# Loads of sixteen rows per partition in three buffers, three chunks held back, tail stores in halves of four rows

## The chip, the cores and the metric

The kernel runs on one core of one Trainium2 chip. The metric is the device time of one execution, in microseconds. The core has TensorE (PE, with its weight loads as PEld), VectorE (DVE), ScalarE (ACT), GpSimd (POOL) and SyncE (SP), and sixteen DMA engines. Two DMA queues matter here: q0, fed by POOL, and q1, fed by SP. Both run on the same sixteen engines.

## What is computed

```python
# _attn_ref, then _moe_ref on its output; B, N, C = 4, 6208, 256; capacity = 128, F = 1024
qn = q / (np.linalg.norm(q, axis=1, keepdims=True) + 1e-06)
kn = k / (np.linalg.norm(k, axis=1, keepdims=True) + 1e-06)
s = kn.transpose(0, 2, 1) @ qn / tau          # 256 x 256 for each batch
a = softmax(s)                                # over the last axis
x = v @ a                                     # 6208 x 256 for each batch
scores = np.einsum('bsd,d->bs', x, w_gate)
for b in range(B):                            # the 128 rows with the largest scores
    top_idx = np.argpartition(-scores[b], capacity)[:capacity]
    xe = x[b, top_idx]
    ye = np.maximum(xe @ w1, 0.0) @ w2
    out[b, top_idx] = xe + sigmoid(scores[b, top_idx])[:, None] * ye   # other rows: out = x
```

## The kernel before, in words

A batch has 6208 rows of 256 floats. They are cut into six chunks of 1024 rows, eight rows (RPP) on each of 128 partitions, and a remainder of 64 rows. POOL's DMAs bring q, k and v in and turn them from f32 into bf16 on the way (`emit_load`); one such load is one chunk of one tensor, 1 MB read and 512 KB written. Output chunks are written by SP's DMAs from f32 stage buffers (`emit_store`), 1 MB each. Batches are numbered 0 to 3; the code calls the last one L and the one before it E.

For each batch TensorE first makes `g_ps` (L390, column norms of q and k, as products of 64 columns with themselves, two side by side) and `s_ps` (L401, k transposed times q). A chain of small steps makes the softmax (`softmax_stages`), which gives `a_sb` and the scoring vector `aw_sb`. TensorE transposes v in groups of four rows (L500), the result is copied to `vt_sb` (13 buffers, `VT_BUFS`), scored (L547) and multiplied with `a_sb` into `o_ps` (L581, two rows at a time, a "pair"), and ACT copies each pair to the stage (L592).

`select_stages` finds the 128 best rows by a seven-step search on DVE and TensorE (L648, L666), gathers their rows of v (`vg`, L734, an indirect DMA on q0), and runs the small network on them: transposes (L758), rows times `a_sb` in two layouts (L768, L771, both in one PSUM tile), h (L795), y (L818) and `upd` (L822). An indirect DMA (L836, the "scatter") then writes the 128 rows over what the plain stores of that batch have written, so it waits for those stores to land.

Batch E is special: two of its chunks (`LATE`) are computed last of all, after batch L, and get the network's result added by TensorE (L588, with one-hot rows `late_oh`), so their stores may follow E's scatter. In the text a "late pair" is four matmuls of L581 and four of L588.

The order of all work is decided by a planner in the kernel's own Python, by costs and due times. It fixes each engine's program; on the chip, semaphores do the rest. What matters here: POOL executes loads, gathers and scatters in the order in which they were emitted, SP likewise its stores. Each DMA of POOL also waits for the landing of the DMA of POOL eight places ahead. `AHEAD` (12 us of load time by the planner's reckoning) limits how many loads are emitted ahead. Output chunks of batches E and L, and of the last two chunks of batch 1 (`BACK`), are held back: their stores start only when the load called `GATE` has landed, the last but one piece of v of batch L. From then on the DMA engines carry stores alone.

## Time and profile before

| | |
|---|---|
| median of 3 runs | 260.41 us (260.26 to 263.3) |
| the profiled execution | 261.13 us |
| its span in the trace | 259.1 us |
| PE, DVE, ACT, POOL busy | 81%, 38%, 37%, 22% of the span |
| q0 (loads, gathers, scatters) | 38.93 MB, 75.4% of sixteen engines' time |
| q1 (weights, stores) | 27.53 MB, 26.3% of sixteen engines' time |

The share of a queue is the time of its packets over the span times sixteen engines. Packets overlap a little on an engine, so shares of a full stretch read 1.0 to 1.07. "GB/s" counts written bytes; the loads read twice what they write.

### The profile page before, as it was taken

Reading aid. Unit: us, or ns where it says so; the run is one execution under the profiler, and the core shown is the slowest. Engines: PE = TensorE matmul, PEld = TensorE weight load, DVE = VectorE, ACT = ScalarE, POOL = GpSimd, SP = SyncE. Lnnn points to the kernel's source line nnn. Section 1 sums busy time; section 2 is a strip of 40 time slices with the busy share of each in tenths; the row PEclk is TensorE's granted clock in tenths of the full one; section 3 lists DMA queues with packets and bytes.
Section 4 is the critical chain, followed back from the end, with each engine's and each line's share of the span. In section 5 each row is a group of like instructions: output and inputs, shape, how many; then the busy total and the mean of one; then the engine's idle time right before and its main releaser. Section 6 shows DMA issues by size and latency. Waiting matters only on the chain.

```text
span 259.1 us, 8212 instructions
## 1 busy us (share of the span) xinstructions
PE 210.8 (81%) x3657; PEld 172.2 (66%) x3657; DVE 97.3 (38%) x414; ACT 96.3 (37%) x176; POOL 56.3 (22%) x105
## 2 busy tenths in 40 slices
PE   0386658778999895998848999898999999999581
PEld 0265546666876674786636788787878888887471
DVE  0200004367450055544463023546555264765021
ACT  3800003900116565466400021811023197798430
POOL 8241213123113110220204322213205200010201
PEclk9999997999999997999995999999999999999979
DMA  7999999999999999999999999999999996999994
GB/s 239 256 218 213 214 214 213 213 212 213 213 217 294 314 361 324 245 282 300 359 240 214 212 215 211 215 210 214 214 213 209 214 211 186 414 419 410 398 409 199
DMA packets 16852, 66.97 MB, mean 259 GB/s; under 512 B 2097, under 2 KB 3634, under 8 KB 13618
## 3 DMA queue, kind: packets, MB, share of 16 engines
q0 software_dynamic: 12528, 38.93, 75.4%
q1 hardware_dynamic: 4290, 27.53, 26.3%
q8 instruction: 28, 0.46, 0.6%
q14 instruction: 6, 0.05, 0.0%
HBM read 78.91 MB, written 25.95 MB: 405 GB/s over the span
## 4 chain that ended last, share of the span: by engine, by line
DMA 43%; PE 37%; DVE 6%; ACT 5%; issue 4%; POOL 1%; SPq 1%; POOLq 1%; DVEq 0%
DMA k_ch<-in_k_dram 18%; DMA q_ch<-in_q_dram 15%; PE s_ps L401 10%; DMA v_ch<-in_v_dram 7%; PE g_ps L390 6%; PE o_ps L581 5%; PE sc_ps L533 4%; ACT stage L592 3%; DMA out_dram<-stage 2%; PE sc_ps L547 2%; PE vt_ps L500 2%; PE m_ps L666 2%; DVE cmp L648 1%; SPq L604 1%; PE g_ps L581 1%
## 5 line engine op out<-in xcount | busy, mean ns | idle before, releaser
L592 ACT COPY stage<-o_ps 128x512 f32<-128x512 f32 x78 | 44.0, 590 | 60.8 <-PE o_ps L581 59.3
L401 PE MATMUL s_ps<-q_ch,k_ch 128*128 128x256 bf16 x384 | 49.9, 283 | 0.0
L581 PE MATMUL o_ps<-a_sb,vt_sb 128*128 128x256 bf16 (+1 forms) x270 | 39.5, 277 | 2.0 <-ACT stage L592 1.9
L401 PEld LDWEIGHTS <-k_ch 128*128 128x128 bf16 x384 | 36.5, 101 | 6.1
L581 PEld LDWEIGHTS <-vt_sb 128*128 128x128 bf16 (+1 forms) x294 | 26.7, 98 | 8.3 <-issue 4.1
L390 PE MATMUL g_ps<-q_ch 128*64 128x64 bf16 x768 | 18.2, 201 | 13.6 <-DMA q_ch<-in_q_dram 13.6
L390 PEld LDWEIGHTS <-q_ch 128*64 128x64 bf16 x768 | 15.0, 116 | 18.8 <-DMA q_ch<-in_q_dram 15.1
L500 PE MATMUL vt_ps<-ident_b,v_ch 128*128 128x128 bf16 x344 | 24.3, 219 | 2.4 <-ACT vt_sb L516 2.3
L390 PE MATMUL g_ps<-k_ch 128*64 128x64 bf16 x768 | 18.3, 202 | 9.2 <-DMA k_ch<-in_k_dram 9.0
L415 DVE SCALAR_TENSOR_TENSOR junk<-g_ps,ident_h 128x64 f32<-128x64 f32 x16 | 3.6, 224 | 58.2 <-PE g_ps L390 57.7
L500 PEld LDWEIGHTS <-v_ch 128*128 128x128 bf16 x384 | 22.7, 97 | 3.7 <-issue 2.5
L390 PEld LDWEIGHTS <-k_ch 128*64 128x64 bf16 x768 | 15.2, 117 | 13.6 <-DMA k_ch<-in_k_dram 10.3
L243 POOL DMA_DIRECT2D q_ch<-in_q_dram x25 | 13.9, 556 | 45.7 <-PE o_ps L581 11.9
L519 DVE COPY vt_sb<-vt_ps 128x1024 bf16<-128x1024 bf16 x24 | 15.8, 688 | 17.4 <-PE vt_ps L500 17.4
L243 POOL DMA_DIRECT2D v_ch<-in_v_dram x25 | 13.6, 545 | 34.6 <-DMA q_ch<-in_q_dram 18.6
L243 POOL DMA_DIRECT2D k_ch<-in_k_dram x25 | 13.7, 546 | 28.3 <-DMA v_ch<-in_v_dram 13.1
L410 ACT COPY s_sb<-s_ps 128x512 f32<-128x512 f32 x4 | 2.3, 585 | 46.8 <-PE s_ps L401 46.8
L533 PE MATMUL sc_ps<-w_sb,ident_b 128*128 128x256 bf16 x123 | 18.5, 277 | 0.4 <-DVE sc L619 0.4
L648 DVE SCALAR_TENSOR_TENSOR cmp<-sc,wl,tab 128x392 bf16<-128x392 f32 x28 | 17.5, 627 | 1.0
L836 POOL DMA_INDIRECT out_dram<-upd,idx x4 | 4.0, 995 | 50.1 <-DMA out_dram<-stage 40.2
L547 PEld LDWEIGHTS <-vt_sb 128*128 128x128 bf16 (+1 forms) x294 | 10.1, 96 | 5.6 <-issue 2.2
L547 PE MATMUL sc_ps<-aw_sb,vt_sb 128*128 128x2 bf16 (+1 forms) x294 | 11.3, 164 | 3.0 <-DVE aw_sb L479 2.5
(176 smaller groups left out, 262.4 us busy)
## 6 DMA issues: line engine op xcount, KB each, us to landing
out_dram<-stage SPq DMA_DIRECT2D x18, 1024.0 KB, 10.3
q_ch<-in_q_dram POOLq DMA_DIRECT2D x23, 512.0 KB, 15.8
k_ch<-in_k_dram POOLq DMA_DIRECT2D x23, 512.0 KB, 17.1
v_ch<-in_v_dram POOLq DMA_DIRECT2D x23, 512.0 KB, 17.5
out_dram<-stage SPq DMA_DIRECT2D x12, 512.0 KB, 8.3
stage<-in_moe_w_dram SPq DMA_DIRECT2D x2, 1024.0 KB, 7.0
q_ch<-in_q_dram POOLq DMA_DIRECT2D x2, 256.0 KB, 16.2
k_ch<-in_k_dram POOLq DMA_DIRECT2D x2, 256.0 KB, 15.9
```

The costliest lines, as they stand in the source:

```text
L243: ins = nc.gpsimd.dma_start(out=t[:, rows, :], in_=lview(src, b, d)[:, rows, :])
L390: nc.tensor.matmul(g_ps[h * H:(h + 1) * H, 2 * which + cc, :], lhsT=x, rhs=x, start=d == FIRST and s == 0 and cc == 0 and which == 0, stop ...
L401: nc.tensor.matmul(s_ps[:, cc, :], lhsT=kt[:parts, s, cc * P:(cc + 1) * P], rhs=qt[:parts, s, :], start=d == FIRST and s == 0 and cc == 0, ...
L500: nc.tensor.transpose(vt_ps[:, cc, j, :parts], in_=vt[:parts, v0 + j, cc * P:(cc + 1) * P], identity=ident_b[:parts, :parts])
L519: nc.vector.tensor_copy(vt_sb[:, :, :n, :parts], vt_ps[:, :, :n, :parts])
L533: nc.tensor.matmul(t[:, 256:512], lhsT=ident_b, rhs=w1_sb[:, 0, 0:256], start=not sc_open[0], stop=not sc_open[0])
L547: nc.tensor.matmul(sc_ps[:parts, col, :], lhsT=vt_sb[:, cc, j, :parts], rhs=aw_sb[:, cc, :], start=cc == 0 and col == 0, stop=cc == 1 and ...
L581: nc.tensor.matmul(o_ps[:parts, pj, :], lhsT=vt_sb[:, cc, j, :parts], rhs=a_sb[:, cc, :], start=pj == 0 and cc == 0, stop=last and cc == 1 ...
L592: nc.scalar.copy(st[:parts, s0 + pair * 2:s0 + pair * 2 + m, :], o_ps[:parts, :m, :])
L648: nc.vector.scalar_tensor_tensor(out=cmp, in0=sc[:, :, None].to_broadcast([P, NCOL, NTHR]), scalar=wl[:, i, NTHR:NTHR + 1], in1=tab[:, Non ...
L666: nc.tensor.matmul(mps[:, 0:7 * NTHR], lhsT=ones_b, rhs=cmp[:, 7 * h:7 * h + 7, :].rearrange("p s j -> p (s j)"), start=h == 0, stop=h == 6)
L836: ins = nc.gpsimd.indirect_dma_start(out=out_flat[0:(b + 1) * N, :], out_offset=bass.IndirectOffsetOnAxis(ap=idx[:, 0:1], axis=0), in_=upd ...
```

## The change

Loads bring sixteen rows per partition (`LR`): three loads in place of six per tensor and batch, each 2 MB read and 1 MB written, with 3 buffers each for q, k and v (5, 5 and 6 of half the size before). The first load of the program and the last ones of batch L stay cut in pieces (8 and 8 rows; 8, 4 and 4 rows). `VT_BUFS` goes from 13 to 9. Three chunks of batch 1 are held back for the time after `GATE`, not two. While E's scoring vector is ready and E's gather not yet emitted, loads are emitted 6 us ahead, not 12. For batches 0 and 1 the norms are products of 128 columns (one matmul for two). Stores of batch L and of the two late chunks go out in halves of four rows on all 128 partitions, each as soon as its two pairs are staged; before, L's halves were 64 partitions of eight rows, after the whole chunk. Late pairs no longer wait for E's scatter to be emitted, only their stores do. The network's second product (`x_ps`) gets a PSUM tile of its own. For batch L the copy `excl_b` goes to DVE. `calm` lets E's network start at a shorter queue.

```diff
-LR = 8
+LR = 16
@@
-    VT_BUFS = 13
+    VT_BUFS = 9
@@
-    BACK = order[-2:]
+    BACK = order[-3:]
@@ pump
-            if not slots[bucket(u)] or sum(length[key] for key in flying) >= AHEAD:
+            ahead = 6.0 if E in aw_ready and E not in gathered else AHEAD
+            if not slots[bucket(u)] or sum(length[key] for key in flying) >= ahead:
@@ p1_norms
+        if b < TILED:
+            for s in range(r0, r1):
+                for cc in range(2):
+                    x = t[:parts, s, cc * P:(cc + 1) * P]
+                    nc.tensor.matmul(g_ps[:, 2 * which + cc, :], lhsT=x, rhs=x,
...
@@
+    def split(b, ci):
+        return ci < NFULL and (b == L or late(b, ci))
...
-            ins = nc.sync.dma_start(out=view(out, b, ci)[h:P:parts], in_=st[h:P:parts])
+            ins = nc.sync.dma_start(out=view(out, b, ci)[:, rows, :], in_=st[:, rows, :])
@@ select_stages
-        by_act = eng.t["act"] < f + 0.5
+        by_act = b < L and eng.t["act"] < f + 0.5
@@
-                                 rhs=vgt[:, cc, :], start=dc == 0 and cc == 0, stop=False)
+                                 rhs=vgt[:, cc, :], start=dc == 0 and cc == 0, stop=dc == 1 and cc == 1)
+        f = eng.pe(4, P, f)
+        which, x_ps = out_psum(None)
         for cc in range(2):
-            nc.tensor.matmul(mps[:, C:2 * C], lhsT=vgt[:, cc, :], rhs=a_sb[:, cc, :], start=False,
+            nc.tensor.matmul(x_ps[:, 0, :], lhsT=vgt[:, cc, :], rhs=a_sb[:, cc, :], start=cc == 0,
                              stop=cc == 1)
@@
-        yield ("t", hfs[0])
+        yield ("calm", hfs[0])
@@ after the scatter
+        if b == E:
+            for x in waiting:
+                out_store(*x)
@@ calm
-            return L in aw_ready or not acc_dead[0] and len(queue["p1"]) > 24
+            return L in aw_ready or not acc_dead[0] and len(queue["p1"]) > 8
@@ out_store
+        if late(b, ci) and E not in scatter_inst:
+            waiting.append((b, ci, s0))
+            return None
...
+        if split(b, ci):
+            rows, size = slice(s0, s0 + 4), STORE / 2 + 0.03
@@ main loop
-                    r = max(r, late_add[2] if E in scatter_inst else FAR)
+                    r = max(r, late_add[2] if late_add else FAR)
@@
-            cost = {1: 0.2, 2: 0.44, 3: 0.44}
+            cost = {1: 0.2, 2: 0.44, 3: 0.88 if out_at < len(outs) and late(outs[out_at][0], outs[out_at][1][0]) else 0.44}
```

The first place is POOL's program from the last pieces of q and k of batch L to the end (`vg` is a gather, `out_dram<-upd` a scatter; "128x2048" is eight rows per partition). Before:

```order
L243 DMA k_ch<-in_k_dram 128x1024
L734 DMA vg<-in_v_dram,idx 128x256
L243 DMA v_ch<-in_v_dram 128x2048
L245 DMA v_rem<-in_v_dram 64x256
L243 DMA v_ch<-in_v_dram 128x2048 x4
L243 DMA v_ch<-in_v_dram 128x1024 x2
L836 DMA out_dram<-upd,idx 12416x256
L734 DMA vg<-in_v_dram,idx 128x256
L836 DMA out_dram<-upd,idx 18624x256
L836 DMA out_dram<-upd,idx 24832x256
```

The same place of the changed kernel:

```order
L246 DMA k_ch<-in_k_dram 128x1024
L246 DMA v_ch<-in_v_dram 128x4096
L754 DMA vg<-in_v_dram,idx 128x256
L248 DMA v_rem<-in_v_dram 64x256
L246 DMA v_ch<-in_v_dram 128x4096
L246 DMA v_ch<-in_v_dram 128x2048
L246 DMA v_ch<-in_v_dram 128x1024 x2
L754 DMA vg<-in_v_dram,idx 128x256
L856 DMA out_dram<-upd,idx 12416x256
L856 DMA out_dram<-upd,idx 18624x256
L856 DMA out_dram<-upd,idx 24832x256
```

E's gather stood ahead of all v loads of L and now stands behind the first of them; L's gather stood behind the scatter of batch 1 and now stands ahead of it.

The second place is SP's program from the remainder of batch E to the end. Before:

```order
L606 DMA out_dram<-stage_rem 64x256
L604 DMA out_dram<-stage 128x2048 x5
L604 DMA out_dram<-stage 64x2048 x2
L606 DMA out_dram<-stage_rem 64x256
L604 DMA out_dram<-stage 64x2048 x10
L604 DMA out_dram<-stage 128x2048 x2
```

And of the changed kernel:

```order
L626 DMA out_dram<-stage_rem 64x256
L624 DMA out_dram<-stage 128x2048 x5
L624 DMA out_dram<-stage 128x1024 x4
L626 DMA out_dram<-stage_rem 64x256
L624 DMA out_dram<-stage 128x1024 x12
```

The twelve halves of batch L and the four of the two late chunks have four rows on 128 partitions now; the late ones still come last.

The third place is the end of TensorE's program: where the second product of L's network (`y`, L818, now L838) stands against the late pairs (`late_oh`). Before, the last rows are:

```order
L588 LDWEIGHTS late_oh
L588 MATMUL g_ps<-d_b,late_oh 128x256
L818 LDWEIGHTS h_sb
L818 MATMUL o_ps<-w_sb,h_sb 128x256
L818 LDWEIGHTS h_sb
L818 MATMUL o_ps<-w_sb,h_sb 128x256
```

Of the changed kernel:

```order
L838 LDWEIGHTS h_sb
L838 MATMUL g_ps<-w_sb,h_sb 128x256
L598 LDWEIGHTS vt_sb
L598 MATMUL o_ps<-a_sb,vt_sb 128x256
L598 LDWEIGHTS vt_sb
L598 MATMUL o_ps<-a_sb,vt_sb 128x256
L605 LDWEIGHTS late_oh
L605 MATMUL o_ps<-d_b,late_oh 128x256
```

Before, all eight late pairs stood ahead of y, five of them ahead of the network and three between its steps. Now three stand ahead of the network, none between its steps, and five behind y.

## Rows read from the trace of the kernel before

**Rows 1.** The page's slices: share of the sixteen DMA engines in tenths.
```profile
DMA  7999999999999999999999999999999996999994
```
**Rows 2.** Stretches: us, busy time of PE, PEld, DVE, ACT, POOL, PEclk, DMA share, GB/s.
```profile
22.00:38.00 16.00, 10.01 (x272) 8.32 (x264) 0.00 (x0) 0.00 (x0) 3.72 (x7) 1.00 1.06 214
201.00:206.00 5.00, 5.00 (x97) 3.97 (x95) 0.82 (x7) 0.00 (x0) 1.58 (x3) 1.00 1.11 214
220.00:229.00 9.00, 8.93 (x132) 7.37 (x130) 6.78 (x25) 7.01 (x14) 0.00 (x0) 1.00 0.99 411
238.00:250.00 12.00, 8.12 (x69) 6.70 (x66) 1.69 (x8) 4.09 (x7) 1.98 (x2) 0.90 1.03 409
```
**Rows 3.** Stretches in which the DMA engines were not full, and the last.
```profile
214.00:219.00 5.00, 4.63 (x76) 3.99 (x73) 1.54 (x7) 3.74 (x9) 0.00 (x0) 1.00 0.55 131
252.00:255.00 3.00, 1.60 (x15) 1.18 (x13) 1.29 (x4) 0.71 (x3) 0.60 (x1) 1.00 0.52 218
257.00:259.10 2.10, 0.00 (x0) 0.00 (x0) 0.00 (x0) 0.00 (x0) 0.00 (x0) 0.69 0.06 21
```
**Rows 4.** Chain that ended last, its end: start us, us, what.
```profile
245.49 6.38 DMA out_dram<-stage
...
252.25 1.92 issue
```
**Rows 5.** Timeline of L's network: start, us, engine, line, output, count, idle before.
```profile
239.05 0.99 POOL L734 DMA_INDIRECT vg<-in_v_dram,idx  x1 [7.07 <-DMA out_dram<-stage_rem]
246.82 0.28 PE L758 MATMUL vt_ps<-ident_b,vg 128*128 128x128 bf16 x2 [3.88 <-DMA vg<-in_v_dram,idx]
249.16 0.42 DVE L776 CAST xet<-m_ps 128x256 bf16<-128x256 f32 x1 [1.72 <-PE m_ps L771]
250.62 0.78 PE L795 MATMUL s_ps<-xet,w_sb 128*128 128x128 bf16 x8
252.56 1.04 PE L818 MATMUL o_ps<-w_sb,h_sb 128*128 128x256 bf16 x8
253.64 0.48 DVE L822 SCALAR_TENSOR_TENSOR upd<-o_ps,gate,xe 128x256 f32<-128x256 f32 x1 [0.80 <-PE o_ps L818]
```
**Rows 6.** DMA issues of the gathers: us from issue to landing last.
```profile
vg<-in_v_dram,idx POOLq DMA_INDIRECT x4, 7.8
```
**Rows 7.** Timeline: the first held store, the scores' end, ACT's copy, the list of rows.
```profile
217.56 0.33 SPq L604 DMA_DIRECT2D out_dram<-stage  x1
222.49 0.15 DVE sc L617
237.02 0.29 DVE L705 TENSOR_SCALAR oh<-iota_row,m_ps 128x128 bf16<-128x128 f32 x1 [0.60 <-ACT excl_b L703]
238.63 0.15 DVE L728 TENSOR_SCALAR idx<-tok 128x1 int32<-128x1 f32 x1
```
**Rows 8.** Timeline of late pairs, at the full and the low clock.
```profile
238.53 0.38 PE L588 MATMUL o_ps<-d_b,late_oh 128*128 128x256 bf16 x2
238.75 0.38 PE L581 MATMUL o_ps<-a_sb,vt_sb 128*128 128x256 bf16 x2
249.34 0.63 PE L588 MATMUL o_ps<-d_b,late_oh 128*128 128x256 bf16 x2
249.77 0.63 PE L581 MATMUL o_ps<-a_sb,vt_sb 128*128 128x256 bf16 x2
248.00:250.00 2.00, 2.00 (x14) 1.50 (x13) 0.76 (x3) 0.58 (x1) 0.00 (x0) 0.50 1.02 430
```
**Rows 9.** Norms of eight rows, and sixteen products of 128 columns, in the chain.
```profile
169.90 0.92 PE vt_ps L500 x16
195.14 0.62 PE g_ps L390 x32
```
**Rows 10.** POOL around E's gather, and TensorE's last product of q and k.
```profile
195.05 1.00 POOL L734 DMA_INDIRECT vg<-in_v_dram,idx  x1 [6.68 <-DVE tokl L741]
204.96 1.05 PE L401 MATMUL s_ps<-q_ch,k_ch 128*128 128x256 bf16 x8
```

More of the change, by code (lines that the diff above doesn't have):

```diff
@@ L183 @@
     FIRST, LAST = lorder[0], lorder[-1]
+    TILED = 2
     L = B - 1
@@ L209 @@
     units = []
+    aw_ready = {}
+    gathered = set()
     for b in range(B):
@@ L352 @@
     scatter_inst = {}
-    gathered = set()
+    split_inst = []
+    waiting = []
+    THROTTLE = 99
     softmaxes = [0]
@@ L385, in p1_norms @@
         parts = P if d < NL else REM
+        if b < TILED:
[3 more added lines that the diff above has]
+                    nc.tensor.matmul(g_ps[:, 2 * which + cc, :], lhsT=x, rhs=x,
+                                     start=d == FIRST and s == 0 and cc == 0 and which == 0,
+                                     stop=d == LAST and s == LR - 1 and cc == 1 and which == 1)
+            return eng.pe(2 * (r1 - r0), P)
         for s in range(r0, r1):
@@ L411, in softmax_stages @@
         sf = eng.act(2 * C, dep)
[L412 removed]
+        junk = smx.tile([P, P], F32, name="junk")
         nsq = smx.tile([P, 4], F32, name="nsq")
         for i in range(4):
[L415 removed]
+            nc.vector.scalar_tensor_tensor(out=junk[:, 0:width(b)], in0=g_ps[:, i, :], scalar=1.0,
+                                           in1=ident_f if b < TILED else ident_h,
                                            op0=ALU.mult, op1=ALU.mult, accum_out=nsq[:, i:i + 1])
[L417 removed]
+            f = eng.dve(width(b), dep, extra=0.08)
         acc_free[0] = max(sf, f)
@@ L801, in select_stages @@
                 nc.scalar.activation(hv, h_ps, AF.Relu)
-                f = eng.act(4 * P, f)
+                hfs.append(eng.act(4 * P, f))
             else:
                 nc.vector.tensor_scalar_max(hv, h_ps, 0.0)
-                f = eng.dve(4 * P, f)
-            bank_give(which, f)
-            hfs.append(f)
+                hfs.append(eng.dve(4 * P, f))
+            bank_give(which, hfs[-1])
         gate = moe.tile([P, 1], F32, name="gate")
@@ L914, in stage_ready, with after, out_store @@
         return rings.landing(("st",) + key)
-    def out_store(b, ci):
+    def after(later, earlier, reason):
+        tc.add_manual_dep(
+            later.ins, earlier.ins.name,
+            mybir.DependencyInfo(mybir.DependencyClass.Sync, mybir.DependencyReason.DATA), reason=reason)
+    def out_store(b, ci, s0):
+        if late(b, ci) and E not in scatter_inst:
+            waiting.append((b, ci, s0))
+            return None
         dep = stage_done[(b, ci)]
@@ L921, in out_store @@
             dep = max(dep, rings.landing(("scatter", E)))
-        parts = (2 if b == L else 1) if ci < NFULL else 1
-        for h in range(parts):
-            key = ("st", b, ci) if h == parts - 1 else ("st", b, ci, h)
-            issued = eng.issue("sp", 0.42, dep)
-            rings.add(1, issued + 0.65, STORE / parts + 0.009 if ci < NFULL else 0.2, key, 0.45)
-            ins = emit_store(b, ci, h, parts)
-        stored[b].append(key)
-        if not late(b, ci):
-            held[b] -= 1
+        if split(b, ci):
+            rows, size = slice(s0, s0 + 4), STORE / 2 + 0.03
+        else:
+            rows, size = slice(0, RPP), STORE + 0.009 if ci < NFULL else 0.2
+        key = ("st", b, ci) if s0 or not split(b, ci) else ("st", b, ci, 0)
+        if split(b, ci) and len(split_inst) >= THROTTLE:
+            dep = max(dep, rings.landing(split_inst[-THROTTLE][1]))
+        issued = eng.issue("sp", 0.42, dep)
+        rings.add(1, issued + 0.65, size, key, 0.45)
+        ins = emit_store(b, ci, rows)
+        if split(b, ci):
+            if len(split_inst) >= THROTTLE:
+                after(ins, split_inst[-THROTTLE][0], "few stores at a time ahead of the last gather")
+            split_inst.append((ins, key))
+        if s0 or not split(b, ci):
+            stored[b].append(key)
+            if not late(b, ci):
+                held[b] -= 1
         return ins
@@ L951 @@
         if deferred and GATE in load_inst:
-            for b, ci in sorted(deferred, key=lambda d: -d[0]):
-                st = out_store(b, ci)
+            for b, ci, s0 in sorted(deferred, key=lambda d: -d[0]):
+                st = out_store(b, ci, s0)
                 if not gate_done:
                     gate_done.append(1)
-                    tc.add_manual_dep(
-                        st.ins, load_inst[GATE].ins.name,
-                        mybir.DependencyInfo(mybir.DependencyClass.Sync, mybir.DependencyReason.DATA),
-                        reason="stores behind the last loads")
+                    after(st, load_inst[GATE], "stores behind the last loads")
             deferred = []
@@ L1063 @@
                     vt_slots.append(f)
-            if out_at == len(outs) or outs[out_at][1][0] != g[0]:
-                if back(b, g[0]) and not gate_done:
-                    deferred.append((b, g[0]))
-                else:
-                    out_store(b, g[0])
+                if split(b, g[0]) or out_at == len(outs) or outs[out_at][1][0] != g[0]:
+                    s0 = g[1] if split(b, g[0]) else 0
+                    if back(b, g[0]) and not gate_done:
+                        deferred.append((b, g[0], s0))
+                    else:
+                        out_store(b, g[0], s0)
 _INS = ['q', 'k', 'v', 'tau', 'moe_w_gate', 'moe_w1', 'moe_w2', 'moe_capacity']
```

29 lines of the change are left out of this document (14 added, 15 removed).

## Prediction

> **What bounds the kernel now.** I read the page's slices first: the sixteen DMA engines show 9 tenths or more in all slices but the first, one at about 217 us and the last [rows 1]. So the program is DMA-bound nearly throughout, and the next thing to know is the rate and the holes. The table of stretches gives the rate: while loads run alone, 214 GB/s written, which is 428 GB/s read; while stores run alone, 409 to 411 GB/s [rows 2]. A load of eight rows (512 KB written) thus takes 0.524 / 214 = 2.45 us, a chunk's store (1.049 MB) 2.55 us. The holes are two. Between 214 and 219 us the share is 0.55, so 2.25 us are lost: the loads run out, and the held stores start only when `GATE` has landed, the first of them at 217.56 [rows 3, 7]. Between 252 and 255 us the share is 0.52, so 1.44 us are lost [rows 3].
>
> The end of the chain says why the second hole is there: the last store of batch L lands at 251.87, the scatter's waits are over at 252.25, and 1.92 us follow in which nothing in the trace holds POOL [rows 4]. The timeline shows that L's `upd` ends only at 253.64 + 0.48 = 254.12, which is what the scatter was short of [rows 5]. So at the very end two things run side by side: the held stores on the DMA engines, and a chain of latencies from the last load over the scores (222.49), the list of rows (238.78), the gather (239.05, landed 246.82) and the network (254.12) [rows 5, 7]. The chain is about 2 us the longer one. What shortens it beyond 2 us gives nothing, since the stores then end last.
>
> The profiled execution took 261.13 us for a span of 259.1, so 2.0 lie outside the span; it stands 0.7 above the median of 260.41. I work in the span and carry the difference to the median.
>
> **The third chunk held back.** One store of 2.55 us moves behind `GATE`. The bytes before it are fewer by 2.55 us, so `GATE` lands at about 215.0, and everything that hangs on it comes 2.55 us earlier. The stores behind it are longer by the same 2.55 us. L's stores therefore still land at about 251.9, but L's network now ends by 251.6, ahead of them. The scatter can start at 252.3 and the 1.44 us hole closes. This is the term that carries the forecast: **-1.4**. The hole at 214 to 219 stays: the stores still wait for the last but one piece of v, four rows as before.
>
> **The network's chain.** L's list of rows also loses ACT's turn, for which DVE stood idle 0.60 us [rows 7]; a DVE copy takes its place, so I take 0.4. Between xet's end (249.16 + 0.42) and h's start (250.62) 1.04 us pass with a late pair on TensorE, and L771 is waited for too [rows 5]; with both out of the way I take 1.5, between 1.0 and 2.1 (the same again for the pair ahead of L768). E's network lies between the gate and L's scores; its gather now lands behind the first third of v. Before, the scores ended 222.49 - 217.56 = 4.9 us behind the gate; I take 0.5 off, with bounds 0 and 2. L's gather took 7.8 us [rows 6] among stores of 8 KB packets; with packets of half the size its eight rows per engine could wait 8 x 0.16 = 1.3 us less (0.16 is half of 2.55 us over eight packets per engine). Nothing of before shows it, so I take none, with the bound 1.3. L's y then ends at 253.60 - 2.55 - 0.4 - 1.5 - 0.5 = 248.65.
>
> **The late pairs behind y.** Five of eight now follow y on TensorE. A pair is four steps of 0.22 us, 0.88, at the full clock, and four of 0.43, 1.72, at the granted clock of 0.50 (1.2 GHz) [rows 8]. Five take 4.4, to 253.05; ACT's copy adds 0.6, the store's start about 1.4 (the first held store was issued at 217.56, and the engines are full again only behind the stretch that ends at 219 [rows 2, 3, 7]), its 512 KB 1.28: 256.3. Without any wait the data would end at 257.1 - 1.44 = 255.7 (257.1 is where the last stretch's 0.06 of 2.1 us ends [rows 3]). So the late pairs end 0.6 behind that. The bound above is worked out under the second rival, the bound below is no wait; with the gather's possible 1.3 in mind I take **+0.3**.
>
> **Sixteen rows per load.** The stretch 201 to 206 has half loads among its DMAs (2 KB written per packet), 22 to 38 whole ones (4 KB): both 214 GB/s [rows 2]. Larger packets would follow that line: no gain. The fastest stretch shown is 430 [rows 8], 0.5% above the 428 that loads read, which on 72 loads x 2.45 = 176 us would be 0.9. I take half, **-0.4**.
>
> The Trainium skill ("DMA: Bandwidth & Descriptors", Anatomy of one DMA and Measured) gives each DMA a fixed 2.0 us beside its bytes and asks for 1 MiB and more per DMA; by it 36 fewer loads would save up to 72 us. The trace disagrees where several loads are in flight: whole loads and half loads move the same 214 GB/s, so the fixed part is hidden, and by the rows the sum stays as it is.
>
> **The stores' halves.** 409 against 411 GB/s between stretches with halves and whole chunks [rows 2], though those halves still had 8 KB packets. 0.5% of eight chunks (20.4 us) is **+0.1**; nothing to 0.4.
>
> **Edits at nothing.** The 128-column norms cost 0.92 - 0.62 = 0.30 us per eight rows of q or k [rows 9], 12.1 times per batch, 7.3 us in two batches. TensorE is idle 6 us of the 16 between 22 and 38 [rows 2], waiting for loads; were that cover gone, a batch would pay 3.6. Fewer `vt_sb` buffers make the last transposes of a batch wait for its first output pairs, which fall beside loads. The moves on POOL: before, E's gather was issued at 195.05 and held POOL 6.68 us, while the queue still had loads up to the last q and k at 204.96, some 9 us [rows 10]. The changed order puts a load of 4.9 us more ahead of it, so the search may end later by about 5 us before the engines run dry.
>
> **Sum.** -1.4 + 0.3 - 0.4 + 0.1 = -1.4: span 257.7, this execution 259.7, median **259.0**.
>
> **Rivals.** *The loads get faster than any stretch here.* If packets of 8 KB cut a fixed time per packet that halves and wholes of today hide, the loads could gain as much as 2%, 3.5 us of 176, and `GATE` comes earlier by that: 259.0 - 3.1 = 255.9. For it: nothing in the rows; against it: the equal 214 GB/s. *The late pairs become the end (slower than before).* The point from which they decide is y at 255.7 - 1.4 - 1.28 - 0.6 - 4.4 = 248.0. If no step of the network gets shorter, y ends at 253.60 - 2.55 = 251.05 and the data at 258.7, 1.6 later than before: 262.0. If TensorE is at its low clock besides, as it was at 248 to 250 after it had waited 3.88 us for the gather [rows 5, 8], the five pairs take 8.6 and the data end at 262.9: 266.2. For it: TensorE has less to do during the gather, since only three pairs stand ahead of it. Against it: the clock was back when y ran (1.04 for its eight products [rows 5]). *The loads stall.* If E's search slips by more than the cover, POOL stands at E's gather with four loads of v behind it, and each us of it is a us of the program; a slip of 8 us costs 3: 262. For it: larger loads in three buffers, nine `vt_sb`. Against it: POOL waited 6.68 us before and the engines stayed full [rows 1, 10]. *It changes nothing:* the hole of 1.44 us moves to the late pairs: 260.4.
>
> **Chances.** The forecast (257.5 to 260) 0.5; no change (260 to 261) 0.15; faster loads 0.13, of which 0.05 below 255.2; late pairs 0.13, of which 0.04 above 265.6; a stall 0.09, of which 0.03 above 265.6. The range 255.8 to 262.5 leaves out about 0.07 below and 0.12 above. About 2% (5.2 us) is what a measurement of this kernel can tell from no change: faster 0.05, slower 0.07, the same 0.88. The likeliest case alone: 257.5 to 260.
>
> **What the changed profile would show.** The first held store at 215.0, 2.5 earlier; loads still at 214 GB/s in a stretch of loads alone; no hole between L's last store and its scatter, and the scatter right behind that store's landing; L's gather landing in 6.5 to 7.8 us; y before 249; the late pairs behind it at 0.88. Wrong would be a DMA share below 1 between 20 and 210 us, or ACT's last copy of a late pair later than 254.5 with idle DMA engines ahead of it.

## The result, and the profile after

The changed kernel takes 263.9 us (median; 263.69 to 264.39), against 260.6 for the kernel before in the same series: a ratio of 1.0109, 95% interval 1.0069 to 1.0150. It is slower by 1.1%: less than the 2% that the prediction took as the least difference it could tell from none, but with an interval that lies clear of 1, and outside the predicted range of 255.8 to 262.5. The profiled execution took 263.74 us for a span of 261.7.

The page's slices, to be laid beside [rows 1]:

```profile
DMA  7999999999999999999999999999997799999966
```

The hole at about 217 us is no longer seen. Instead there are two sevens at 196 to 209 us, and the last two slices stand at six. Stretches of the changed kernel (columns as in [rows 2]):

```profile
22.00:38.00 16.00, 10.95 (x126) 10.32 (x127) 0.00 (x0) 0.00 (x0) 1.58 (x3) 0.79 1.04 216
200.00:205.00 5.00, 4.88 (x127) 3.85 (x120) 4.00 (x23) 0.20 (x1) 2.07 (x4) 1.00 0.35 67
214.00:219.00 5.00, 4.91 (x81) 4.21 (x78) 2.31 (x9) 3.47 (x8) 0.00 (x0) 1.00 0.96 263
252.00:255.00 3.00, 3.00 (x28) 2.70 (x29) 0.63 (x2) 1.17 (x2) 0.96 (x1) 1.00 0.36 147
257.00:261.70 4.70, 0.00 (x0) 0.00 (x0) 0.00 (x0) 0.54 (x1) 0.00 (x0) 0.99 0.57 227
```

Loads alone run at 216 GB/s (214 before). The hole at 214 to 219 us shrank from 2.25 us [rows 3] to 0.2. But 200 to 205 us, where [rows 2] show full engines, now loses 3.25 us (0.65 of 5). The hole that was to close, 252 to 255 us, grew from 1.44 us to 1.92. And where before almost nothing moved behind 257 us [rows 3], 2.7 us of transfers are left. (Holes are counted against a share of 1.00. Full stretches of loads read up to 1.11, as [rows 2] show, and not only up to 1.07, so these losses are lower bounds.)

The first hole has its cause on POOL. Timeline of DVE, POOL and SP around E's search and gather, first held store, and the end of L's scores:

```profile
183.17 0.15 DVE L637 TENSOR_REDUCE sc<-sc_ps 64x1 f32<-64x2 f32 x1 [0.44 <-PE sc_ps L564]
202.50 0.15 DVE L748 TENSOR_SCALAR idx<-tok 128x1 int32<-128x1 f32 x1
202.93 1.00 POOL L754 DMA_INDIRECT vg<-in_v_dram,idx  x1 [16.68 <-DVE tokl L761]
204.43 2.32 POOL L246 DMA_DIRECT2D v_ch<-in_v_dram  x4
216.32 2.26 SPq L624 DMA_DIRECT2D out_dram<-stage  x2
223.70 0.15 DVE L637 TENSOR_REDUCE sc<-sc_ps 64x1 f32<-64x2 f32 x1 [0.44 <-PE sc_ps L564]
```

POOL stood 16.68 us at E's gather (6.68 before [rows 10]) with one remainder and four loads of v behind it. The gather went out 7.9 us later than before, and 7.2 of these are the start of the search, at 183.17. In the kernel before, the search began at 176.00, and the last transposes ahead of it stood on TensorE at 173.62:

```profile
173.62 1.05 PE L500 MATMUL vt_ps<-ident_b,v_ch 128*128 128x128 bf16 x16
176.00 0.15 DVE L617 TENSOR_REDUCE sc<-sc_ps 64x1 f32<-64x2 f32 x1 [0.44 <-PE sc_ps L547]
```

TensorE of the changed kernel at that place:

```profile
175.26 0.61 PE L517 MATMUL vt_ps<-ident_b,v_ch 128*128 128x128 bf16 x8
175.70 1.04 PE L598 MATMUL o_ps<-a_sb,vt_sb 128*128 128x256 bf16 x8
176.57 0.61 PE L517 MATMUL vt_ps<-ident_b,v_ch 128*128 128x128 bf16 x8
...
179.18 1.05 PE L598 MATMUL o_ps<-a_sb,vt_sb 128*128 128x256 bf16 x8
180.06 0.61 PE L517 MATMUL vt_ps<-ident_b,v_ch 128*128 128x128 bf16 x8
180.51 1.04 PE L598 MATMUL o_ps<-a_sb,vt_sb 128*128 128x256 bf16 x8
181.39 0.61 PE L517 MATMUL vt_ps<-ident_b,v_ch 128*128 128x128 bf16 x8
```

Here transposes of E's last groups (L517) and output pairs (L598, which free `vt_sb`) take turns, and norms of the next batch come between (177.64 to 179.18, left out). Before, two groups were transposed at one go. With nine buffers the tenth group of a batch has to wait until a pair has used up one of the first nine.

The second hole and the end: timeline of L's network, with the scatters of batch 1 (241.01), E (248.39) and L (253.98), and ACT's last copy of a late pair:

```profile
239.71 0.99 POOL L754 DMA_INDIRECT vg<-in_v_dram,idx  x1 [32.96 <-DVE idx L748]
241.01 1.00 POOL L856 DMA_INDIRECT out_dram<-upd,idx  x1 [0.30 <-issue]
247.34 0.29 PE L778 MATMUL vt_ps<-ident_b,vg 128*128 128x128 bf16 x2 [4.29 <-DMA vg<-in_v_dram,idx]
248.39 0.97 POOL L856 DMA_INDIRECT out_dram<-upd,idx  x1 [6.37 <-DMA out_dram<-upd,idx]
251.16 1.39 PE L838 MATMUL g_ps<-w_sb,h_sb 128*128 128x256 bf16 x8
252.59 0.48 DVE L842 SCALAR_TENSOR_TENSOR upd<-g_ps,gate,xe 128x256 f32<-128x256 f32 x1 [0.44 <-PE g_ps L838]
253.98 0.96 POOL L856 DMA_INDIRECT out_dram<-upd,idx  x1 [4.62 <-DMA out_dram<-upd,idx]
256.96 0.58 ACT L609 COPY stage<-o_ps 128x512 f32<-128x512 f32 x1 [0.29 <-PE o_ps L605]
```

Two scatters waited for the landing of the one before. And SP waited for E's scatter with the late stores behind it (waits of SP, 236 to 260 us: total, times, longest):

```profile
SPq L624 <- DMA out_dram<-upd,idx: 8.0, 1, 8.0
```

Both signs that the prediction had named as wrong stand in these rows: a share below 1 between 20 and 210 us, and a last copy of a late pair later than 254.5 with idle engines ahead of it.

So three suspects stood: **A**, the nine `vt_sb` buffers make E's scores late, hence the hole on POOL and a later network of E; **C**, the late pairs behind y set the end; **D**, the scatter of batch 1 moved behind L's gather, every scatter waits for the one before, and the late stores wait for E's. The rival of A was the load size, the rival of all of them the third chunk itself. Times of different series are compared by their ratio to the kernel before, which took 260.6 to 261.8 in them.

### The profile page after: what moved, and what is told of

It is laid out like the page before. It is cut to its first block, busy times and chain, and to the rows that moved or that the text cites. A ratio compares the mean times of both kernels' runs of the same rounds, so it can differ in the third digit from the quotient of the medians.

```text
span 261.7 us, 7347 instructions
## 1 busy us (share of the span) xinstructions
PE 215.6 (82%) x3235; PEld 183.7 (70%) x3235; DVE 95.4 (36%) x411; ACT 101.3 (39%) x179; POOL 40.0 (15%) x74
## 3 DMA queue, kind: packets, MB, share of 16 engines
q0 software_dynamic: 8064, 38.93, 72.7%
## 4 chain that ended last, share of the span: by engine, by line
DMA 42%; PE 25%; issue 23%; ACT 3%; POOL 2%; DVE 2%; POOLq 0%; ACTq 0%
DMA q_ch<-in_q_dram 31%; DMA v_ch<-in_v_dram 9%; PE o_ps L598 6%; PE s_ps L417 6%; PE g_ps L406 4%; DMA vg<-in_v_dram,idx 3%; ACT vt_sb L533 2%; PE vt_ps L517 1%; ACT stage L609 1%; PE m_ps L686 1%; PE sc_ps L564 1%; PE sc_ps L550 1%; POOL v_ch L246 1%; PE o_ps L816 1%; PE o_ps L605 1%
## 5 line engine op out<-in xcount | busy, mean ns | idle before, releaser
L598 PE MATMUL o_ps<-a_sb,vt_sb 128*128 128x256 bf16 (+1 forms) x278 | 40.0, 277 | 0.9 <-ACT stage L609 0.6
L417 PEld LDWEIGHTS <-k_ch 128*128 128x128 bf16 x384 | 37.2, 100 | 4.8
L598 PEld LDWEIGHTS <-vt_sb 128*128 128x128 bf16 (+1 forms) x294 | 27.4, 99 | 7.3 <-issue 3.0
L517 PE MATMUL vt_ps<-ident_b,v_ch 128*128 128x128 bf16 x336 | 25.7, 223 | 5.6 <-ACT vt_sb L533 3.4
L517 PEld LDWEIGHTS <-v_ch 128*128 128x128 bf16 x384 | 23.8, 99 | 7.9 <-issue 4.8
L398 PE MATMUL g_ps<-q_ch 128*128 128x128 bf16 x192 | 14.0, 234 | 15.8 <-DMA q_ch<-in_q_dram 15.8
L398 PEld LDWEIGHTS <-q_ch 128*128 128x128 bf16 x192 | 12.3, 105 | 17.1 <-DMA q_ch<-in_q_dram 16.3
L398 PE MATMUL g_ps<-k_ch 128*128 128x128 bf16 x192 | 16.2, 258 | 8.4 <-DMA k_ch<-in_k_dram 8.4
L398 PEld LDWEIGHTS <-k_ch 128*128 128x128 bf16 x192 | 14.8, 119 | 9.4 <-DMA k_ch<-in_k_dram 9.4
L536 DVE COPY vt_sb<-vt_ps 128x1024 bf16<-128x1024 bf16 x16 | 11.0, 691 | 25.4 <-PE vt_ps L517 25.4
L533 ACT COPY vt_sb<-vt_ps 128x1024 bf16<-128x1024 bf16 (+1 forms) x23 | 19.7, 925 | 0.8 <-PE vt_ps L517 0.7
L754 POOL DMA_INDIRECT vg<-in_v_dram,idx x4 | 4.0, 1005 | 104.2 <-DVE idx L748 87.5
L690 DVE TENSOR_REDUCE cnt<-m_ps 128x8 f32<-128x56 f32 x28 | 6.1, 217 | 19.7 <-PE m_ps L686 19.7
L246 POOL DMA_DIRECT2D q_ch<-in_q_dram x15 | 8.7, 578 | 26.5 <-DMA v_ch<-in_v_dram 13.1
L246 POOL DMA_DIRECT2D k_ch<-in_k_dram x15 | 8.3, 554 | 26.8 <-DMA v_ch<-in_v_dram 11.7
```

The costliest lines, as they stand in the source:

```text
L246: ins = nc.gpsimd.dma_start(out=t[:, rows, :], in_=lview(src, b, d)[:, rows, :])
L398: nc.tensor.matmul(g_ps[:, 2 * which + cc, :], lhsT=x, rhs=x, start=d == FIRST and s == 0 and cc == 0 and which == 0, stop=d == LAST and s ...
L417: nc.tensor.matmul(s_ps[:, cc, :], lhsT=kt[:parts, s, cc * P:(cc + 1) * P], rhs=qt[:parts, s, :], start=d == FIRST and s == 0 and cc == 0, ...
L517: nc.tensor.transpose(vt_ps[:, cc, j, :parts], in_=vt[:parts, v0 + j, cc * P:(cc + 1) * P], identity=ident_b[:parts, :parts])
L533: nc.scalar.copy(vt_sb[:, :, :n, :parts], vt_ps[:, :, :n, :parts])
L536: nc.vector.tensor_copy(vt_sb[:, :, :n, :parts], vt_ps[:, :, :n, :parts])
```

## Experiments: one suspect at a time

### The order of loads and E's gather on POOL

```diff
-            ahead = 6.0 if E in aw_ready and E not in gathered else AHEAD
+            ahead = AHEAD
```

> One edit against the changed kernel: loads are emitted 12 us ahead at all times, so one more v load of sixteen rows (4.9 us) stands ahead of the gather of batch 2 on POOL. Theory A (POOL standing at that gather until 202.9 us dries the DMA engines, 3.3 us lost between 198 and 208): the hole closes, the first held store is issued at about 213 instead of 216.3, and the time falls by 2 to 3 us to about 261; the late pairs behind y still end last. Theory B (larger loads and fewer buffers hold the loads back of themselves): the hole stays, only later, and the time stays within 0.7 us of 263.9.

Measured: 264.53 (264.29 to 264.88), ratio 1.0109 (1.0061 to 1.0156). E's gather still goes out at 203.00, but fewer loads stand behind it:

```profile
200.00:205.00 5.00, 4.88 (x130) 3.85 (x122) 4.00 (x22) 0.20 (x1) 2.00 (x3) 1.00 1.03 211
250.00:252.00 2.00, 1.93 (x21) 1.54 (x18) 0.61 (x2) 1.06 (x3) 0.00 (x0) 0.77 0.19 66
258.02 0.59 ACT L609 COPY stage<-o_ps 128x512 f32<-128x512 f32 x1 [0.29 <-PE o_ps L605]
```

Theory A gave a gain of 2 to 3 us, and there is none. The hole is shut (1.03), and the first held store starts at 213.30, 3.0 us earlier. Not one of these 3 us reaches the end: L's scores end at 224.35 (223.70 with the hole), and the engines run empty at 250 us instead, while late pairs are computed until 258. The hole was real, but it was not what ended last.

### The late pairs ahead of L's network

```diff
+                if self.b == L and out_at < len(outs):
+                    return FAR
```

(in `Chain.ready`, under the step that waits for the gather)

> One edit against the changed kernel: the network of the last batch is emitted only when all eight late pairs are, so all stand ahead of it on TensorE, in the 7.6 us in which it waits for the gather. Theory C (the five late pairs behind y end the program: last copy at 257.5, data at 260.0): the hole of some 2.5 us at 251 to 254 closes, the data end at about 258 and the time falls by about 2 us to 262. If the end were set by the stores alone, it stays at 263.9. If the pairs make the network late, the scatter is later than 254.0 and the gain is smaller.

Measured: 263.88 (263.01 to 265.95), ratio 1.0102 (1.0034 to 1.0171). The last copy of a late pair starts at 247.25, 9.7 us earlier than in the changed kernel, and still nothing is gained, where theory C gave 2 us. Stretch, POOL and SP's wait:

```profile
252.00:254.00 2.00, 0.54 (x5) 0.23 (x4) 0.61 (x2) 0.00 (x0) 0.00 (x0) 1.00 0.09 37
249.54 0.97 POOL L856 DMA_INDIRECT out_dram<-upd,idx  x1 [7.73 <-DMA out_dram<-upd,idx]
SPq L624 <- DMA out_dram<-upd,idx: 8.5, 1, 8.5
```

The finished late chunks lie in their stages and wait for E's scatter, which waits for that of batch 1. That speaks for D.

### The scatter of batch 1 ahead of L's gather

```diff
-            return max(...) + (0.5 if L in gathered else 3.0)
+            return max(...) + (0.5 if L in gathered else -6.0 if b < E else 3.0)
```

> Of the changed kernel only the order on POOL at the end is changed: the scatter of batch 1 is issued ahead of L's gather, as in the kernel before, instead of behind it. Theory D (each scatter waits for the landing of the scatter before it, E's late stores wait for E's scatter, so a scatter moved behind L's gather makes the hole of 2.5 us between 250 and 254): the scatter of E is issued by 244 instead of 248.4, the DMA share of 250 to 254 is above 0.85 instead of about 0.45, and the stores are through about 2 us earlier as far as the late pairs let them. Theory C (the three late pairs and more behind y set the end by themselves): the hole closes, ACT's last copy stays at 257.0, and the time stays within 0.6 us of the changed kernel's 263.9. D and no C: 261.9. If D is wrong, the scatter of E stays at 248 or the hole stays with the scatter early.

Measured: 264.92 (263.92 to 265.45), ratio 1.0129 (1.0084 to 1.0175). E's scatter is out at 242.70, and the end is now the late pairs':

```profile
242.70 0.99 POOL L856 DMA_INDIRECT out_dram<-upd,idx  x1 [2.22 <-DMA out_dram<-upd,idx]
258.68 0.59 ACT L609 COPY stage<-o_ps 128x512 f32<-128x512 f32 x1 [0.29 <-PE o_ps L605]
```

The hole does not close but moves back: 250 to 252 us stand at 0.94, 252 to 254 at 0.48, 254 to 256 at nothing.

So C and D hide each other: the late stores need both the late pairs and E's scatter, and whichever is left holds them.

### Two suspects, and all three

The first two edits together:

> Both edits. If A and C hold and are separate, the gains add: 263.9 - 3 - 2 = about 259, under the kernel before (260.6), and the engines are full from 20 us to the scatter but for the hand-over from loads to stores. If they share one hole, the time is that of the better one, 261 to 262.

Measured: 261.30 (260.67 to 262.15), ratio 0.9994 (0.9970 to 1.0018): 1.15% below the changed kernel, where each edit alone gave nothing. What is left is D: E's scatter at 248.98, and 250 to 252 us at 0.19.

All three edits:

> All three suspects are taken out of the changed kernel: the output pairs no longer go ahead of the transposes of E (hole at 200 to 205 us), the late pairs stand ahead of L's network, and the scatter of batch 1 ahead of L's gather. The first two together gave 261.3 with a hole left at 250 to 252 us (share 0.19) and E's scatter at 248.98. Theory D: the hole closes, E's scatter is out by 245, and what is left is the last scatter's wait: 259.3 to 260.2, at or below the kernel before (260.6). If the scatter order is worth nothing beside the other two: 261.3 again.

Measured: 259.64 (259.36 to 260.08), ratio 0.9938 (0.9915 to 0.9960), faster than the kernel before. Its stretches:

```profile
250.00:252.00 2.00, 1.65 (x18) 0.95 (x14) 1.03 (x4) 0.76 (x3) 0.00 (x0) 1.00 1.03 422
252.00:255.00 3.00, 0.00 (x0) 0.00 (x0) 0.37 (x1) 0.00 (x0) 0.97 (x1) 1.00 1.00 403
```

The engines are full from 250 to 255 (245 to 250 stand at 0.80), and no late pair is computed behind 250.

## Experiments: the buffers, the loads and the third chunk by themselves

### Thirteen buffers, and the control

```diff
-    ST_BUFS = 9
-    VT_BUFS = 9
+    ST_BUFS = 8
+    VT_BUFS = 13
```

> The changed kernel with 13 buffers for the transposed rows, as before the change, and 8 instead of 9 for the output tiles, which makes room for them. Theory A (nine buffers make the last four transposes of a batch wait for its output pairs, so E's search starts 7 us late and POOL stands at E's gather with loads of v behind it): E's search starts at about 176 instead of 183, its gather is issued near 195.5 instead of 202.9, the DMA share of 200 to 205 is above 0.9 instead of 0.35, the first held store is at 213 to 214 instead of 216.3, and the scatter of batch 1 is ahead of L's gather again. The third chunk's gain then shows: 260 if nothing else ends it, 262 to 262.5 by theory C, since the late pairs still follow y (as in the kernel with loads of eight rows, 263.5). If the output tiles are the scarce thing instead, the time is 264 or more.

Measured: 261.26 (260.00 to 263.44), ratio 0.9991 (0.9951 to 1.0031). E's search starts at 175.44, its gather goes out at 195.93, the first held store at 214.30, and the planner by itself puts the scatter of batch 1 (231.15) ahead of L's gather (236.68). Theory A holds, and the order behind D is gone with it. That order needs the third chunk too: with nine buffers and two chunks (last run of this section) the planner also puts the scatter of batch 1 first (235.29 against 240.90). C remains, as expected: the last late pair's copy starts at 255.79, and 252 to 254 us stand at 0.14.

The control, output tiles alone:

```diff
-    ST_BUFS = 9
+    ST_BUFS = 8
```

> A control: the changed kernel with 8 output tiles instead of 9 and its 9 buffers for the transposed rows. With 13 of these and 8 of those it took 261.3. Theory A (the buffers of the transposed rows): 263.5 to 265, the hole at 200 to 205 us stays. If the gain came with the output tiles and the order that they bring: 261.3.

Measured: 264.15 (263.49 to 265.33), ratio 1.0105 (1.0052 to 1.0157), with 200 to 205 us at 0.43. The output tiles did not bring the gain.

### The nine buffers in the kernel before

```diff
-    VT_BUFS = 13
+    VT_BUFS = 9
```

> The kernel before with 9 buffers for the transposed rows instead of 13, and nothing else. Its planner then puts E's gather behind five loads of v instead of ahead of them. Theory A: E's search starts at 181 to 184 instead of 176.0, its gather is issued after 201 instead of 195.05, E's network and L's list of rows come later, L's gather at 240 or later instead of 239.05, and the time is 261.2 to 262.5. If the buffers cost nothing, as the prediction had it: the search starts at 176 and the time is 260.6.

Measured: 265.41 (263.69 to 266.05), ratio 1.0136 (1.0083 to 1.0189). That is more than either theory gave. Search, E's gather, first held store, end of L's scores, L's gather, last scatter and the stretch ahead of it:

```profile
188.69 0.15 DVE L617 TENSOR_REDUCE sc<-sc_ps 64x1 f32<-64x2 f32 x1 [0.44 <-PE sc_ps L547]
209.94 1.00 POOL L734 DMA_INDIRECT vg<-in_v_dram,idx  x1 [8.26 <-DVE tokl L741]
217.27 0.33 SPq L604 DMA_DIRECT2D out_dram<-stage  x1
225.64 0.15 DVE L617 TENSOR_REDUCE sc<-sc_ps 64x1 f32<-64x2 f32 x1 [0.46 <-PE sc_ps L547]
242.14 1.00 POOL L734 DMA_INDIRECT vg<-in_v_dram,idx  x1 [2.06 <-DVE idx L728]
258.11 0.98 POOL L836 DMA_INDIRECT out_dram<-upd,idx  x1 [14.97 <-DVE upd L822]
252.00:258.00 6.00, 6.00 (x55) 5.03 (x53) 2.16 (x7) 2.72 (x6) 0.00 (x0) 0.79 0.09 36
```

With loads of eight rows the search slips by 12.7 us. The planner had put five loads of v ahead of the gather, so POOL's queue did not run dry; the price is paid at the other end, where the last scatter waits for `upd` and the engines stand still for 5.5 us. The gate is as early as before (first held store at 217.27; 217.56 [rows 7]), yet L's scores end 3.15 us later (225.64; 222.49 [rows 7]), behind E's network, whose y starts at 222.37 instead of 217.41.

### The loads

The kernel before with the large loads and the nine buffers that make room for them:

```diff
-LR = 8
+LR = 16
-    VT_BUFS = 13
+    VT_BUFS = 9
```

> The kernel before with loads of sixteen rows in three buffers, and 9 buffers for the transposed rows, which makes the room; two chunks kept back, no halves, all late pairs as before. Loads at 216 to 217 GB/s instead of 213 to 214 give 1.5 to 2 us over 176 us; theory A takes some back: E's search at 181 or later, a hole at 200 to 205 us where POOL stands at E's gather with loads of v behind it. Theory A: 261.5 to 264. Loads alone, if the buffers cost nothing: 258.6 to 259.2.

Measured: 261.69 (259.69 to 264.77), ratio 1.0014 (0.9985 to 1.0043). That is the lower edge of theory A's range and far from the 258.6 to 259.2 of the loads alone. But the hole that theory A gave is not there (200 to 205 us at 1.05; two loads of v and the remainder stand ahead of E's gather), and the runs spread over 5 us, with the profiled one the fastest of them. E's search starts at 183.34, 5.4 us earlier than with eight rows and nine buffers, so part of the difference to the run above is order, not rate.

The changed kernel with loads of eight rows and 13 buffers:

```diff
-LR = 16
+LR = 8
-    VT_BUFS = 9
+    VT_BUFS = 13
```

> The changed kernel with loads of eight rows and thirteen vt_sb buffers again; all else stays, the third held chunk, the halves of four rows, the 128-column norms, the late rule. Theory A: the search of batch 2 starts at about 176 as before, POOL's wait does not dry the engines, and the hole at 198 to 208 is gone; with six late pairs behind y the end is still later than it need be: 259.5 to 261.5. If the time stays near 264, the loads and buffers are not what cost the time.

Measured: 263.55 (262.16 to 266.58), ratio 1.0073 (1.0039 to 1.0108). No hole at 200 to 205 (E's gather at 195.33), scatter of batch 1 at 228.46; late pairs are copied until 256.0. This is a miss: theory A gave 259.5 to 261.5, and a time near 264 was to clear the loads and buffers. With C still there the run by itself tells neither. Against 0.9991 with large loads and 13 buffers this hints that the large loads are worth something; the cleaner run follows below.

### The third chunk

```diff
-    BACK = order[-3:]
+    BACK = order[-2:]
```

> The changed kernel with two chunks of batch 1 kept back, as before the change; all else of the change stays (loads of sixteen rows, nine buffers, halves, five late pairs ahead of L's network and three behind it). Theory that the third chunk itself costs the time (more late pairs and a scatter behind L's gather): 260.6 or less, as before the change. Theory A (the buffers' hole at 200 to 205, 3.3 us, is there as well): the first held store at 218.5 to 219.5, the time 261.5 to 263, most of the loss stays.

Measured: 264.01 (263.83 to 264.35), ratio 1.0107 (1.0065 to 1.0149), the changed kernel's ratio within 0.0002, and above both forecasts. The first held store is at 218.47, 2.15 us later than with three chunks, and the end does not move. But this pair differs in more than the chunk: the scatter of batch 1 stands ahead of L's gather, three late pairs and not five stand behind y, and E's gather goes out at 204.52 and not at 202.93. The chunk's own price is read from a cleaner pair below.

## Experiments: the same terms in a kernel without the losses

13 buffers and the late pairs ahead of L's network:

```diff
-    ST_BUFS = 9
-    VT_BUFS = 9
+    ST_BUFS = 8
+    VT_BUFS = 13
@@
+                if self.b == L and out_at < len(outs):
+                    return FAR
```

> The changed kernel with 13 buffers for the transposed rows (8 for the output tiles), and with L's network emitted only when all late pairs are. The first edit alone gave 261.3 with a hole of 2.7 us at 250 to 254 (shares 0.49 and 0.14), while ACT's last copy of a late pair ended at 256.4. Theory: those are theories A and C, and D is served by the first edit, since the scatter of batch 1 then stands ahead of L's gather. The hole closes, L's last scatter waits for L's stores only (252), and the time is 258.0 to 259.2, clearly below the kernel before (260.6). Rival, that the late pairs ahead of L's network push y and the last scatter later by as much as they save: 260.5 to 261.5.

Measured: 261.24 (260.26 to 262.38), ratio 0.9994 (0.9968 to 1.0020): a miss. In the profiled execution the end is as it should be (full until 256), but E's gather, which stands ahead of all loads of v there, goes out at 197.77, and 196 to 200 us stand at 0.38: 2.5 us lost on POOL. (With 13 buffers alone it had gone out at 195.93, and the share was 0.85, 0.6 us lost. Both kernels issue the same work in the same order up to there, and E's search began at 175.44 in that execution, at 177.90 in this one, the slowest of its ten: the loss at the gather differs from one execution to the next.) The next run puts the first load of v ahead of that gather, by this edit more:

```diff
-            ahead = 6.0 if E in aw_ready and E not in gathered else AHEAD
+            ahead = AHEAD
```

> As the kernel before in this list, and one load of v more issued ahead of E's gather on POOL. In the kernel with 13 buffers alone POOL still stood at that gather, with the DMA share of 196 to 200 at 0.85, which is 0.6 us. If that hole is on the path: 0.4 to 0.8 less than without this edit, 257.5 to 258.6. If E's network comes later by as much as the loads come earlier (as in the kernel where this edit stood alone): the same or 0.3 more.

Measured: 259.23 (258.92 to 259.29), ratio 0.9914 (0.9875 to 0.9953), faster than the kernel before by 0.9%. I had given the hole 0.4 to 0.8, from an execution that lost little there; it was worth 2.1. From here three terms of the change were undone one at a time.

**Late pairs behind y again** (the two lines of `return FAR` taken out):

```diff
-                if self.b == L and out_at < len(outs):
-                    return FAR
```

> The fastest version so far (259.2) with the late pairs where the change put them, five of them behind y. Theory C by itself: ACT's last copy at 255 to 256 and the DMA engines partly idle at 250 to 254, 260.6 to 261.5. If the late pairs are hidden: 259.2.

Measured: 261.76 (260.89 to 262.56), ratio 1.0014 (0.9986 to 1.0042): 1.0%, 2.6 us slower. 250 to 252 us stand at 0.13, the last copy starts at 256.11.

**Loads of eight rows again:**

```diff
-LR = 16
+LR = 8
```

> The fastest version so far (259.2) with loads of eight rows, as before the change. It measures the larger loads by themselves. By the rates read so far (216 to 217 against 213 to 214 GB/s while loads run alone, 1 per cent of 176 us): 260.5 to 261. If larger packets bring nothing, 259.2; the prediction took 0.4: 259.6.

Measured: 260.76 (260.53 to 261.07), ratio 0.9979 (0.9953 to 1.0005): 0.65%, 1.7 us slower. The edit also brings back the load buffers of before (5, 5 and 6 of half the size) and the cuts of the last loads. Loads alone read 213 GB/s there in the stretch of 22 to 38 us and 215 in the kernel with large ones, but 213 in both from 164 to 190. The first held store is at 214.29 instead of 213.08.

**Two chunks held back again:**

```diff
-    BACK = order[-3:]
+    BACK = order[-2:]
```

> The fastest version so far (13 buffers for the transposed rows, late pairs ahead of L's network, loads ahead of E's gather as before the change; 259.2) with two chunks of batch 1 kept back instead of three. It measures the term that carried the prediction, where nothing hides it. The prediction's theory (the chain behind the gate ends last, so 2.55 us of stores moved behind the gate shorten the end by 1.4): 260.4 to 260.8. Rival (the stores end last there, the third chunk only changes places with them): 259.0 to 259.5. It would be below 258.9 if the third chunk costs something by itself.

Measured: 258.99 (258.66 to 260.48), ratio 0.9921 (0.9893 to 0.9949): the same, by the rival's forecast. First held store, end of L's scores and L's gather, first with three chunks, then with two:

```profile
213.08 1.03 SPq L624 DMA_DIRECT2D out_dram<-stage  x2
221.38 0.15 DVE L637 TENSOR_REDUCE sc<-sc_ps 64x1 f32<-64x2 f32 x1 [0.44 <-PE sc_ps L564]
237.50 0.99 POOL L754 DMA_INDIRECT vg<-in_v_dram,idx  x1 [6.71 <-DVE idx L748]
```

```profile
215.41 0.99 SPq L624 DMA_DIRECT2D out_dram<-stage  x2
221.47 0.15 DVE L637 TENSOR_REDUCE sc<-sc_ps 64x1 f32<-64x2 f32 x1 [0.44 <-PE sc_ps L564]
237.47 0.99 POOL L754 DMA_INDIRECT vg<-in_v_dram,idx  x1 [6.88 <-DMA out_dram<-stage]
```

The gate comes 2.33 us earlier with the third chunk, L's scores end 0.09 earlier, and L's gather moves by 0.03. (In both kernels the last scatter, at 251.31 and 251.23, waits for a store, so the time alone would not show a shorter chain here; the rows do.) What L's scores hang on is TensorE. In the second of the two kernels E's y and the last of L's scores read

```profile
214.36 1.26 PE L838 MATMUL o_ps<-w_sb,h_sb 128*128 128x256 bf16 x8
221.08 0.35 PE L564 MATMUL sc_ps<-aw_sb,q_ch 128*128 128x2 bf16 x8
```

and between them eight groups of transposes and their scores follow one another, about 6 us of TensorE work behind E's network. The planner put the network ahead of them, and no landing of v within that stretch is waited for.

## Why the prediction was wrong, point by point

**"Everything that hangs on it comes 2.55 us earlier", the -1.4.** The first half is right: the third chunk moves the first held store by 2.15 us (216.32 against 218.47) and 2.33 (213.08 against 215.41). The second half is the first step that failed. I took the scores' end as a fixed 4.9 us behind the gate because the rows stood so [rows 7]. In the changed kernel it was 7.4 (223.70 - 216.32), in the last pair of runs 8.3 and 6.1, and in the kernel before with nine buffers 8.4, with the gate where it was. The list of L follows E's network on TensorE, not the gate. The chain of the kernel before, read from 195 us to the end of the scores, could have told it: it runs through TensorE's products, the softmax, E's network and the scores, and no landing of a load is among its longest pieces. Two of them, E's y and the scores:

```profile
217.41 1.10 PE o_ps L818 x8
222.28 0.19 PE sc_ps L547 x8
```

In the clean pair the term is nothing; the bytes only change places. No run holds the third chunk back in the kernel before, where the chain still ended last; that it would gain nothing there follows from these rows, not from a time.

**"Fewer `vt_sb` buffers ... fall beside loads", at nothing.** This is the largest error. I asked what the waiting transposes cost TensorE and not what waits for their scores. The search, a chain of some 19 us (183.17 to 202.50), starts when the last transpose is scored; the gather follows it, and four loads and E's network follow the gather. 13 buffers take back 1.1% against their control (3.0 us), nine alone cost the kernel before 1.4% (3.5 us).

**"The moves on POOL", at nothing up to a slip of 5 us.** The rival "the loads stall" described what happened: the slip was 7.9 us, the hole 3.25, for which it gave 3 (262). It had 0.09, although I named the nine `vt_sb` as a reason for it. Its price, an end at 262, is not what the runs show: the run that shut the hole alone gained nothing, since other waits covered it. The same order on POOL costs 2.1 us even with 13 buffers, where the search began at 177.90 (0.9994 against 0.9914).

**The network's chain.** Here the sizes were right. The gather took 7.6 us (239.71 to 247.34 with its wait; 6.5 to 7.8 forecast). From there to the end of `upd` 5.73 us pass, against 7.30 before [rows 5]: 1.57, where I took 1.5. From the scores' end to the list 15.59 us pass against 16.14 [rows 7]: 0.55, where I took 0.4. But y ended at 252.55 and not at 248.65, since the chain began late: L's gather went out at 239.71 and not at 235.60 (239.05 - 2.55 - 0.4 - 0.5), and all of that comes from the scores' end.

**The late pairs, +0.3.** Speed right (0.87 each, 0.88 forecast), start wrong by y's 3.9 us, so ACT's last copy ended at 257.54 instead of 253.65. With y at 248.0 as the point from which they decide, the rival was the likelier case once the chain did not come earlier. In a kernel without the other losses they cost 2.6 us.

**What I did not see: the scatters.** The order rows showed that L's gather had moved ahead of the scatter of batch 1, and I named it without costing it. What was queued behind it were two more scatters, each waiting for the one before, and all late stores. It costs 0.56%, 1.5 us, where the other two suspects are gone (0.9994 against 0.9938), and nothing where both are left.

**Loads of sixteen rows, -0.4.** Right in sign, too small: 1.7 us. The stretch of loads alone reads 216 GB/s against 214 [rows 2], which over 176 us would be 1.6; but from 164 to 190 us it is 214 against 213, so the rate gives a part at most, and where the rest comes from is not shown. The rival of faster loads was half right; its 2% stood on no row. The Trainium skill ("DMA: Bandwidth & Descriptors", Anatomy of one DMA) states a fixed part of about 2.0 us per DMA, from which the prediction's estimate was up to 72 us. The runs differ from that: 36 fewer loads gave 1.7, so with several loads in flight nearly all of a fixed part is hidden.

**The norms at nothing** agrees with the traces: TensorE is idle 5 us of the 16 between 22 and 38 (10.95 busy, at a granted clock of 0.79) and waits for loads. The norms, **the stores' halves, +0.1**, `calm` and the PSUM tile of `x_ps` were not tried by themselves.

So the sum failed by +4.9 (263.9 against 259.0): a gain that was not there (1.4), a loss costed at nothing that let two others through, and a gain of 1.3 more than I took on the loads. The losses do not add up, since they cover one another: taking one away gained 0.0, 0.1 and -0.2%, all three together 1.7%.

## What to carry to other kernels

A distance between two events in a trace is a dependence only if the second waits for the first; before moving an event, look at what the second really waited for, here an engine's queue and not the gate. When buffers are cut, follow the last of the waiting instructions to whoever waits for its result, above all to a search or gather that holds up a queue of loads. Where three waits end close together, undoing one of them shows nothing; undo them together, and then put each back alone.

## What was not expected of the hardware

Loads of 2 MB in three buffers (8,064 packets on the load queue instead of 12,528) move 216 GB/s between 22 and 38 us where loads of 1 MB moved 214, although in both cases several loads are in flight. In the fastest kernel the large loads, with their buffers, are worth 1.7 us, which that rate does not explain in full, as said above.

The hole where loads end and held stores begin is smaller when the loads have stalled shortly before. In the six runs that lost 2 us or more at E's gather, the six us from 214 to 220 stand at 0.86 to 0.99, so at most 0.8 us are lost (2.25 before, from 214 to 219); in the fastest kernel, without that stall, it is back (1.6 us, 210 to 214 at 0.60):

```profile
210.00:214.00 4.00, 3.54 (x65) 3.10 (x66) 2.38 (x10) 3.96 (x8) 0.00 (x0) 1.00 0.60 125
```

This row is of the fastest kernel with three chunks held back. Why a stall narrows that hole was not tried.

A scatter of 128 rows among full stores took some 7 us from issue to landing (241.01 to 248.39 in the changed kernel, and the next could not start before), where its 128 KB would be 0.3 us at the 411 GB/s of the stores.
